# First blocks of a fused Mamba-2 scan and ELU layer: exponents from three bf16 parts, a shorter first load, a later state

## The chip, the cores and the metric

The kernel runs on one core of a Trainium2 chip. A core has TensorE (matrix products, "PE" in the profile, its weight loads "PEld"), VectorE ("DVE"), ScalarE ("ACT"), GpSimd ("POOL"), and SyncE ("SP"), which here issues nearly all DMA transfers. The metric is the device time of one execution in microseconds (us), median of three. The profile describes one execution and has its own clock: its span runs from the first to the last instruction.

## The reference

First a state-space scan over 4 batches, 8 heads and 768 tokens, with head dimension 32 and state dimension 16, in chunks of 32 tokens; then a two-layer network with ELU over the 3072 tokens (256 to 2048 to 256).

```python
log_a = np.log(np.clip(a, 1e-06, 1.0))
for c in range(nc):                                  # chunks of one sequence
    cum = np.cumsum(la, axis=-1)
    L = np.exp(cum[..., :, None] - cum[..., None, :]) * causal
    M = np.einsum('bhin,bhjn->bhij', Cc, Bc) * L
    y_intra = np.einsum('bhij,bhjd->bhid', M, xc)
    y_inter = np.einsum('bhin,bhnd->bhid', Cc, state) * np.exp(cum)[..., None]
    y[:, :, sl] = y_intra + y_inter
    decay_from_j = np.exp(cum[..., -1:] - cum)
    state = np.exp(np.sum(la, -1))[..., None, None] * state + sum_j(Bc * xc * decay_from_j)
h = x @ w_in                                         # x is y, heads side by side
g = np.where(h > 0.0, h, np.exp(np.minimum(h, 0.0)) - 1.0)
out = g @ w_out
```

The result does not depend on the chunk length. The weights come as 64-bit floats and are made 32-bit on the chip.

## The kernel before: the parts concerned

The kernel uses chunks of 64 tokens (`Q`) and blocks of 256 tokens of one batch, so there are 12 blocks. Index `u` is a half block of 128 tokens, `v` a chunk in it, `q` a pair of heads. All instructions stand in the order in which the program writes them; each engine takes its own in that order.

The logarithm of a, its running sum within chunks (`F[:, 0]`), the exp of that (`F[:, 1]`), and the decay to the end of a chunk (`E`) are made once for all blocks, on 96 rows (the last 32 of 128 repeat the first):

```python
la = const.tile([P, 2, P], F32, name="la")
for k, g in enumerate((0, 1, 2, 0)):
    (nc.scalar if k % 2 else nc.sync).dma_start(out=la[BH * k:BH * (k + 1)], in_=...)   # cut
...
nc.vector.tensor_scalar(out=la, in0=la, scalar1=1e-6, scalar2=1.0, op0=ALU.max, op1=ALU.min)
nc.scalar.activation(la, la, ACT.Ln)
nc.vector.tensor_tensor_scan(out=F[:, 0]..., data0=keep..., data1=la..., ...)           # cut
nc.scalar.activation(F[:, 1], F[:, 0], ACT.Exp)
nc.vector.tensor_tensor(out=E..., in0=F_uv[:, :, Q - 1:Q].to_broadcast(...), in1=F_uv, op=ALU.subtract)
nc.scalar.activation(E, E, ACT.Exp)
```

The exponents of L for blocks 0 and 1 are made on TensorE, in a PSUM bank for each half of the heads, from a mask (`first_low`), plus the running sum along one axis (`first_cum`), minus it along the other (`first_minus`), in 32-bit products of 32 rows; `first_decay` takes their exp. Later blocks get L through a copy in DRAM (`write_flat`, `spread_cum`) and 16 small exps (`decay`).

```python
def first_cum(*which):
    for k in range(4):
        for n, hh, r in which:
            row, rows = 32 * r + rows_of(n).start % 32 + 4 * hh + k, slice(32 * r, 32 * r + 32)
            for v in range(2):
                nc.tensor.matmul(out=st[n]["x", hh][Q * v:Q * v + Q, k],
                    lhsT=ident[rows, row:row + 1].to_broadcast([32, Q]),
                    rhs=F[rows, 0, :, Q * v:Q * v + Q], ...)

def first_minus(*which):
    for u in range(2):
        for n, hh, r in which:
            ...
            nc.tensor.matmul(out=st[n]["x", hh][:, :, u], lhsT=F[rows, 0, u],
                rhs=minus[rows, r0:r0 + 4].unsqueeze(2).to_broadcast([32, 4, Q]), ...)
```

The other steps of a block: `turned(E, "eb", ...)` turns E so that tokens are rows; `scaled` multiplies B by it on GpSimd (`sc`); `turn` turns B and C on TensorE (`bt`, `ctm`); `first_exp` spreads `F[:, 1]` (`ec`), which `turn_exp` multiplies into C (`cts`); `sums` makes the chunks' additions to the state, `states` the states (`S_new` on VectorE, masked `Sx` on GpSimd); `scores` makes C times B in four banks; `weigh(n, q)` multiplies a bank by L (`M`, VectorE); `across` and `inside` make y in four banks, and end with ScalarE's copies to `yT`.

```python
def weigh(n, q):
    M = att.tile([P, 2, 2, Q], F32, tag="M", name="M", bufs=8)
    nc.vector.tensor_tensor(out=M, in0=s["g"][q], in1=s["L"][:, 2 * q:2 * q + 2]..., op=ALU.mult)
```

The network: `l1(n, i)` makes two of 16 column blocks of the hidden layer, `elu()` its ELU (two ScalarE passes over `e`, one VectorE operation that writes `g` and is the last reader of the PSUM bank), `l2(n, j)` the second layer.

```python
def l1(n, i):
    ps = psum([P, 2, BLK], "ps_h")
    for j in range(2):
        m = 2 * i + j
        for k in range(KC):
            nc.tensor.matmul(out=ps[:, j], lhsT=w_in[:, k, m * P:(m + 1) * P], rhs=yT[n // 2]..., ...)

def elu():
    n, i, ps = lag.pop(0)
    nc.scalar.activation(e, ps, ACT.Relu, scale=-1.0)
    nc.scalar.activation(e, e, ACT.Exp, scale=-1.0)
    nc.vector.scalar_tensor_tensor(out=g_of[n][:, 2 * i:2 * i + 2], in0=e, scalar=1.0, in1=ps,
                                   op0=ALU.subtract, op1=ALU.max)
```

A weight piece is one load of 512 KB (`w_load`), an Abs and a low part on ScalarE (`w_abs`, `w_low`), a sign, a clamp and a shift on VectorE (`w_sign`, `w_high_a`, `w_high_b`), and a sum on GpSimd (`w_sum`). From piece 4 the low part is VectorE's. `l1(n, i)` needs piece i.

[...] Seven form a ring of buffers (tag "a"), taken in turn; one is kept apart for `l2`, the idle products and some sums. The order of the first blocks:

```python
first = (0, 0, 0), (0, 1, 3)
first_low(0, 0); first_low(0, 1); idle_products(3)
first_cum(*first)
eb = turned(E, "eb", 1.0, nc.scalar)
turn(0); first_exp(0); scaled(0, nc.gpsimd); turn_exp(0)
sums(0, pool=p_o, tag="o")
first_minus(*first)
w_abs(0); first_decay(0, 0); w_low(0, nc.scalar); first_decay(0, 1)
states(0)
for _ in range(2):
    psum([P, 4, P], "ps_none")
scores(0)
w_sign(0); w_high(0); w_sum(0)
for q in range(4):
    weigh(0, q)
second = (1, 0, 0), (1, 1, 3)
first_low(1, 0); first_low(1, 1, p_o)
w_abs(1); w_low(1, nc.scalar)
inside(across(0), 0)
w_sign(1); w_high_a(1); w_sign(2); w_high_b(1); w_sum(1)
l1(0, 0)
w_abs(2); w_low(2, nc.scalar); w_give(2)
first_cum(*second); first_minus(*second)
l1(0, 1); elu()
w_abs(3); w_sign(3); w_low(3, nc.scalar)
first_decay(1, 0); first_decay(1, 1)
turn(1); first_exp(1); scaled(1, nc.gpsimd); w_give(3); turn_exp(1)
l1(0, 2); elu()
scores(1)
sums(1, pool=p_o, tag="o")
weigh(1, 0); weigh(1, 1)
elu()
states(1)
weigh(1, 2); weigh(1, 3)
l1(0, 3)
w_take(4, nc.vector)
inside(across(1), 1)
ncum = turned(F[0:ROWS, 0], "ncum", -1.0, nc.vector)
w_give(4); elu()
...                     # loads cut; then l1 of (1, 0), (1, 1), (0, 4), (1, 2), (0, 5), (1, 3), (0, 6),
                        # (1, 4), (0, 7), (1, 5), (1, 6), (1, 7), with block 2 and pieces 5 to 9 between
ends = {(3, 14): 4, (5, 10): 6, (7, 13): 8, (9, 9): 10}   # (block, step) after which y of two blocks is made
```

After that, `l2(n - 2, i)` and `l1(n, i)` alternate for n from 2 to 11, with the scan of the later blocks between.

## Time and profile before

| | us |
|---|---|
| time, median of 3 runs | 387.92 |
| time, lowest and highest | 387.64, 389.07 |
| span of the profiled execution | 385.5 |
| w_in piece 0: issued, landed | 4.7, 9.6 |
| L of block 0: the two exps end | 10.78, 11.91 |
| last products (second half of the second layer, block 11) start | 368.5 |

In a line of the timeline the columns are the start, the time to the end of the group, the engine, the source line, the operation, output and inputs, the count, and, in brackets, how long the engine had been idle and what ended that. A line of groups with a count is a run of equal instructions. A 32-bit matrix product is two records of the trace; a bf16 product is one. The page names `l1` as L538, `l2` as L569, `first_cum` as L368, `first_minus` as L379, `scores` as L417, the yT copies as L521, `weigh` as L426 and the VectorE part of `elu` as L552.

The weights and the scan's inputs are loaded by long runs of small transfers, most of them in the first 60 us:

```profile
w<-in_moe_w_in_dram SPq DMA_DIRECT2D x8, 512.0 KB, 5.2
xr<-in_x_dram SPq DMA_DIRECT2D x24, 128.0 KB, 3.2
bc<-in_B_dram SPq DMA_DIRECT2D x24, 64.0 KB, 3.7
```

The columns are the transfer, the issuing queue, the number of transfers, the size of one, and the median time from issue to landing.

### The profile page before, as it was taken

How to read it: one execution, taken by the hardware profiler on the slowest of the kernel's cores; microseconds unless marked ns; L12 is line 12 of the kernel's file. 1: busy time of each engine (PE TensorE's matmuls, PEld its weight loads, DVE VectorE, ACT ScalarE, POOL GpSimd, SP SyncE). 2: the span in 40 equal slices, each digit the busy share in tenths (PEclk: the TensorE clock that was granted, in tenths of full speed). 3: DMA queues.
4: the chain of work that ended last, by engine and by line, in shares of the span. 5: the costliest groups of instructions: out<-in, count | busy, mean ns of one | idle time of the engine just before them, and what ended most of it. 6: DMA issues, size and time to landing. Idle time of an engine off the chain costs nothing.

```text
span 385.5 us, 8666 instructions
## 1 busy us (share of the span) xinstructions
PE 378.7 (98%) x3544; PEld 324.1 (84%) x3544; DVE 136.9 (36%) x280; ACT 196.7 (51%) x455; POOL 72.1 (19%) x131
## 2 busy tenths in 40 slices
PE   8899999999999999999999999999999999999996
PEld 4678788888888888888888888888888888888885
DVE  4877878932521232611132431123161212221000
ACT  3969969675334576344467335367534333334000
POOL 5525426623200112400022220011310000000000
PEclk9999999999999999999999999999999999999999
DMA  8979956543004505003524002540000000000000
GB/s 173 226 155 263 296 88 148 96 105 94 3 28 57 84 0 138 3 3 61 64 40 136 3 2 41 60 67 29 0 4 2 27 2 23 4 2 28 0 29 27
DMA packets 87176, 25.15 MB, mean 65 GB/s; under 512 B 77312, under 2 KB 81760, under 8 KB 87136
## 3 DMA queue, kind: packets, MB, share of 16 engines
q1 hardware_dynamic: 84960, 24.39, 29.6%
q8 instruction: 28, 0.46, 0.5%
q10 hardware_dynamic: 2176, 0.20, 0.4%
q14 instruction: 12, 0.10, 0.1%
HBM read 21.23 MB, written 3.34 MB: 64 GB/s over the span
## 4 chain that ended last, share of the span: by engine, by line
PE 88%; ACT 4%; DMA 3%; SPq 3%; issue 1%; DVE 0%; ACTq 0%
PE ps_o L569 40%; PE ps_h L538 38%; PE ps_o L585 4%; PE ps_y L508 2%; SPq L111 2%; PE ps_g L417 1%; DMA w<-in_moe_w_in_dram 1%; PE ps_y L490 1%; ACT L L397 1%; DMA xr<-in_x_dram 1%; PE ps_st L445 1%; DMA flat<-F 1%; ACT e L550 1%; SPq L119 1%; ACT mag L156 1%
## 5 line engine op out<-in xcount | busy, mean ns | idle before, releaser
L538 PE MATMUL ps_h<-yT,w_in 128*128 128x256 f32 x768 | 181.4, 380 | 1.4 <-DVE g L552 0.9
L569 PE MATMUL ps_o<-w_out,g 128*128 128x256 f32 x704 | 166.1, 380 | 0.0
L538 PEld LDWEIGHTS ps_h<-yT,w_in 128*128 128x128 f32 x768 | 145.1, 190 | 22.6 <-ACT yT L521 0.9
L569 PEld LDWEIGHTS ps_o<-w_out,g 128*128 128x128 f32 x704 | 132.3, 190 | 18.2 <-POOL L L402 0.2
L552 DVE SCALAR_TENSOR_TENSOR g<-e,ps_h 128x512 f32<-128x512 f32 x96 | 65.9, 686 | 208.3 <-ACT e L551 208.3
L550 ACT ACTIVATE e<-ps_h 128x512 f32<-128x512 f32 x96 | 57.1, 595 | 138.2 <-PE ps_h L538 138.1
L551 ACT ACTIVATE e<-e 128x512 f32<-128x512 f32 x96 | 60.5, 631 | 3.0
L402 POOL TENSOR_SCALAR_AFFINE_SELECT L<-L 64x512 f32<-64x512 f32 x40 | 27.0, 675 | 157.0 <-ACT L L397 155.6
L397 ACT ACTIVATE L<-L,ncum 128x64 f32<-128x64 f32 x160 | 41.8, 333 | 0.0
L521 ACT COPY yT<-ps_y 64x256 f32<-64x256 f32 (+3 forms) x46 | 14.3, 318 | 9.8 <-PE ps_y L508 9.3
L467 POOL TENSOR_TENSOR Sx<-S_new,hmask 128x64 f32<-128x64 f32 x44 | 13.0, 304 | 20.3 <-DVE S_new L462 12.7
L426 DVE TENSOR_TENSOR M<-ps_g,L 128x256 f32<-128x256 f32 x48 | 16.8, 415 | 0.1
L575 ACT COPY ob<-ps_o 128x512 f32<-128x512 f32 x11 | 6.3, 577 | 15.3 <-PE ps_o L569 15.3
L585 PE MATMUL ps_o<-w_out,g 128*128 128x256 f32 x64 | 14.0, 379 | 0.0
L585 PEld LDWEIGHTS ps_o<-w_out,g 128*128 128x128 f32 x64 | 12.2, 190 | 1.7
L198 POOL TENSOR_TENSOR w_in<-mag,w_in 128x512 uint32<-128x512 uint32 x8 | 10.3, 1294 | 15.8 <-DVE mag L188 15.8
L198 POOL TENSOR_TENSOR w_out<-mag,w_out 128x512 uint32<-128x512 uint32 x8 | 10.2, 1275 | 15.4 <-DVE mag L188 15.4
L188 DVE SCALAR_TENSOR_TENSOR mag<-mag,sgn 128x512 uint32<-128x512 uint32 x16 | 12.6, 790 | 0.5
L462 DVE SCALAR_TENSOR_TENSOR S_new<-S_new,ec,ps_st 128x64 f32<-128x64 f32 x40 | 10.9, 279 | 2.1
L156 ACT ACTIVATE mag<-w 128x512 f32<-128x512 f32 x16 | 10.8, 672 | 1.4 <-DMA w<-in_moe_w_in_dram 1.4
L508 PE MATMUL ps_y<-M,xr 64*32 64x64 f32 x768 | 9.6, 225 | 0.0
L342 DVE TENSOR_TENSOR ctm<-ps_tc,hmask 128x512 f32<-128x512 f32 x12 | 8.2, 684 | 3.8 <-PE ps_tc L335 3.8
(66 smaller groups left out, 132.8 us busy)
## 6 DMA issues: line engine op xcount, KB each, us to landing
L<-flat SPq DMA_DIRECT2D x20, 256.0 KB, 4.7
w<-in_moe_w_in_dram SPq DMA_DIRECT2D x8, 512.0 KB, 5.2
w<-in_moe_w_out_dram SPq DMA_DIRECT2D x8, 512.0 KB, 6.0
xr<-in_x_dram SPq DMA_DIRECT2D x24, 128.0 KB, 3.2
out_dram<-ob SPq DMA_DIRECT2D x11, 256.0 KB, 2.2
bc<-in_B_dram SPq DMA_DIRECT2D x24, 64.0 KB, 3.7
bc<-in_C_dram SPq DMA_DIRECT2D x22, 64.0 KB, 3.0
ec<-flat_exp SPq DMA_DIRECT2D x72, 16.0 KB, 1.7
```

What stands on the lines that cost most here:

```text
L156: nc.scalar.activation(w_mag[i].bitcast(F32), w_words(i)[1].bitcast(F32), ACT.Abs)
L198: nc.gpsimd.tensor_tensor(out=w, in0=w_mag[i][:, :, cols], in1=w, op=ALU.add)
L397: nc.scalar.activation(L[:, h, u], L[:, h, u], ACT.Exp, bias=ncum[:, u, row:row + 1])
L402: nc.gpsimd.affine_select(out=part, in_=part, pattern=[[0, 4], [0, 2], [1, Q]], compare_op=ALU.is_ge, fill=0.0, base=0, channel_multiplier=-1)
L426: nc.vector.tensor_tensor(out=M, in0=s["g"][q], in1=s["L"][:, 2 * q:2 * q + 2].rearrange("p k u i -> p u k i"), op=ALU.mult)
L508: nc.tensor.matmul(out=y[t][v][col:col + D, at, u], lhsT=s["x"][toks, u, D * h:D * (h + 1)], rhs=s["M"][h // 2][toks, u, h % 2], start=Fal ...
L538: nc.tensor.matmul(out=ps[:, j], lhsT=w_in[:, k, m * P:(m + 1) * P], rhs=yT[n // 2][:, k, n % 2].rearrange("p u i -> p (u i)"), start=(k = ...
L550: nc.scalar.activation(e, ps, ACT.Relu, scale=-1.0)
L551: nc.scalar.activation(e, e, ACT.Exp, scale=-1.0)
L552: nc.vector.scalar_tensor_tensor(out=g_of[n][:, 2 * i:2 * i + 2], in0=e, scalar=1.0, in1=ps, op0=ALU.subtract, op1=ALU.max)
L569: nc.tensor.matmul(out=o_of[n][:, ts], lhsT=g_of[n][:, m, ts * P:(ts + 1) * P], rhs=w_out[:, m], start=(m == 0 and ts == 0), stop=(m == MC ...
L585: nc.tensor.matmul(out=ps, lhsT=g_of[n][:, m, ts * P:(ts + 1) * P], rhs=w_out[:, m], start=(m == 0), stop=(m == MC - 1))
```

## The change

The change has five parts. It is meant to let the first y come sooner, and to take work of blocks 0 and 1 out of TensorE's way.

1. The first log a to arrive (`la0`) is that of the first 256 tokens of all rows, loaded four times into the four quarters of the partitions. The full log a follows as one load, and its logarithm, scan, exp and E come later, in the middle of the first blocks.
2. The exponents of blocks 0 and 1 come from `cum16`: bf16(cum) on two quarters of the rows, and the two remainders, each rounded to bf16, on the others. One product over 128 rows adds them up, so `first_cum` and `first_minus` are bf16 products. Those of block 1 move ahead of `across(0)`.
3. The first weight piece is loaded and converted in two halves of 128 columns.
4. The last state of block 0 (chunk `u = v = 1`) is made after block 1's states, ahead of `l1(0, 3)`.
5. PSUM is eight named banks with one buffer each. The first block's tiles name their banks; later ones follow a ring of seven. The steps at which scores, y and some decays of blocks 4 to 11 are made are changed.

```diff
+    banks = ctx.enter_context(tc.tile_pool(name="banks", bufs=1, space=PSUM))
+    ring = [0]
+    def psum(shape, name, bank=None):
+        if bank is None:
+            bank = ring[0]
+            ring[0] = (bank + 1) % 7
+        return banks.tile(shape, F32, tag=f"bank{bank}", name=name)
...
-    nc.vector.tensor_scalar(out=la, in0=la, scalar1=1e-6, scalar2=1.0, op0=ALU.max, op1=ALU.min)
-    nc.scalar.activation(la, la, ACT.Ln)
...
+    clip(la0)
+    nc.scalar.activation(la0, la0, ACT.Ln)
+    sums_of(F0, la0)
+    nc.scalar.copy(out=cum16, in_=F0[:, 0])
+    from_last(E0, F0[:, 0], nc.vector)
+    nc.scalar.activation(E0, E0, ACT.Exp)
+    low2, low3 = slice(2 * BH, P), slice(3 * BH, P)
+    nc.vector.tensor_tensor(out=left[low2], in0=F0[low2, 0], in1=cum16[low2], op=ALU.subtract)
+    nc.vector.tensor_copy(cum16[low2], left[low2])
+    nc.vector.tensor_tensor(out=cum16[low3], in0=left[low3], in1=cum16[low3], op=ALU.subtract)
+    nc.scalar.activation(F0[:, 1], F0[:, 0], ACT.Exp)
...
+    def first_cum(n, hh):
+        for k in range(4):
+            for v in range(2):
+                nc.tensor.matmul(
+                    out=ps[Q * v:Q * v + Q, k],
+                    lhsT=sel[:, row + k:row + k + 1].to_broadcast([P, Q]),
+                    rhs=cum16[:, :, Q * v:Q * v + Q], ...)
+        for u in range(2):
+            nc.tensor.matmul(
+                out=ps[:, :, u], lhsT=cum16[:, u],
+                rhs=minus[:, row:row + 4].unsqueeze(2).to_broadcast([P, 4, Q]), ...)
...                                        # the new order of the first blocks
+    first_low(0, 0, 0)
+    first_low(0, 1, 1)
+    idle_products(3)
+    eb0 = turned(E0, "eb0", 1.0, nc.scalar, BH, 4)
+    turn(0, (5, 6))
+    first_exp(0, 7)
+    scaled(0, nc.gpsimd)
+    turn_exp(0)
+    sums(0, bank=(4, 5), part=most)
+    for hh in range(2):
+        first_cum(0, hh)
+        first_decay(0, hh)
+    states(0, most)
+    scores(0, bank=(6, 7, 0, 1))
+    w_abs(0, half[0])
+    w_low(0, nc.scalar, half[0])
+    weigh(0, 0)
+    weigh(0, 1)
+    w_sign(0, half[0])
+    w_high(0, half[0])
+    w_sum(0, half[0])
+    weigh(0, 2)
+    weigh(0, 3)
+    clip(la)
+    for hh in range(2):
+        first_low(1, hh, 2 + hh)
+        first_cum(1, hh)
+    w_abs(0, half[1])
+    w_low(0, nc.scalar, half[1])
+    nc.scalar.activation(la, la, ACT.Ln)
+    first_decay(1, 0)
+    inside(across(0, bank=(4, 5, 6, 7)), 0)
+    w_sign(0, half[1])
+    w_high(0, half[1])
+    w_sum(0, half[1])
+    w_abs(1)
+    w_sign(1)
+    w_high_a(1)
+    w_low(1, nc.scalar)
+    w_sign(2)
+    w_high_b(1)
+    w_sum(1)
+    sums_of(F, la)
+    nc.scalar.activation(F[:, 1], F[:, 0], ACT.Exp)
     l1(0, 0)
+    first_decay(1, 1)
     w_abs(2)
     w_low(2, nc.scalar)
     w_give(2)
-    first_cum(*second)
-    first_minus(*second)
     l1(0, 1)
     elu()
...                                        # block 1 as before, up to:
     weigh(1, 2)
     weigh(1, 3)
+    st[0] = kept
+    sums(0, bank=(None, 7), part=last)
+    states(0, last)
     l1(0, 3)
     w_take(4, nc.vector)
     inside(across(1), 1)
-    ncum = turned(F[0:ROWS, 0], "ncum", -1.0, nc.vector)
+    from_last(E, F[:, 0], nc.gpsimd)
+    ncum = turned(F[:, 0], "ncum", -1.0, nc.vector, ROWS)
+    nc.scalar.activation(E, E, ACT.Exp)
+    eb = turned(E, "eb", 1.0, nc.scalar, ROWS)
     w_give(4)
     elu()
...
-    ends = {(3, 14): 4, (5, 10): 6, (7, 13): 8, (9, 9): 10}
+    ends = {(3, 8): 4, (5, 10): 6, (7, 6): 8, (9, 10): 10}
+    scores_at = {4: 1, 6: 2, 8: 0, 10: 2}
```

## The prediction

> **What bounds the kernel now.** I read the granted clock first (1.000 on the one core, so nothing is throttled), then the page's first part, then a table of busy time by stage, then the timeline of the first 54 us.
>
> ```profile
> PE 378.7 (98%) x3544; PEld 324.1 (84%) x3544; DVE 136.9 (36%) x280; ACT 196.7 (51%) x455; POOL 72.1 (19%) x131
> ```
>
> 98% says little by itself, because matmul ends are modelled. The chain of waits has 1.73 us for each group of 8 records of the two large layers. There are 12 x 8 groups of each layer, so 192 x 1.73 = 332 us of the 385.5 us is work that nothing here changes. The stage table shows where the rest lies (columns: stretch, length, busy time and count of PE, PEld, DVE, ACT, POOL, clock, DMA share, GB/s):
>
> ```profile
> 0.00:13.65 13.65, 11.11 (x214) 6.30 (x215) 7.95 (x23) 7.55 (x17) 7.25 (x25) 1.00 0.86 179
> 13.65:27.43 13.78, 13.54 (x232) 10.48 (x232) 10.66 (x23) 9.48 (x21) 5.90 (x8) 1.00 0.87 205
> 27.43:53.40 25.97, 24.96 (x262) 20.60 (x263) 19.79 (x43) 21.89 (x54) 12.06 (x15) 1.00 0.93 238
> 53.40:368.50 315.10, 315.10 (x2773) 274.74 (x2772) 98.47 (x193) 156.41 (x364) 46.90 (x83) 1.00 0.22 42
> ```
>
> From 53.4 us on TensorE never idles, so the retimed scores and ends of the later blocks can gain nothing there; they can only cost. Everything is decided by when TensorE reaches the first l2, at 53.42 us. Before that, ScalarE is busy 21.89 of 25.97 us and DVE 19.79: those queues, not TensorE alone, set the pace. The timeline's landmarks (start, duration, engine, line, operation):
>
> ```profile
> 11.40 1.41 DVE L426 TENSOR_TENSOR M<-ps_g,L 128x256 f32<-128x256 f32 x4
> ...
> 13.68 1.97 PE L538 MATMUL ps_h<-yT,w_in 128*128 128x256 f32 x8 [0.21 <-ACT yT L521]
> ...
> 15.57 1.10 PE L368 MATMUL ps_x<-F,ident 32*64 32x128 f32 x32
> ...
> 16.61 1.14 PE L379 MATMUL ps_x<-minus,F 32*128 32x256 f32 x8
> ...
> 17.67 1.99 PE L538 MATMUL ps_h<-yT,w_in 128*128 128x256 f32 x8
> ...
> 22.20 0.69 PE L417 MATMUL ps_g<-ctm,bt 32*64 32x128 f32 x32
> ...
> 23.36 1.99 PE L538 MATMUL ps_h<-yT,w_in 128*128 128x256 f32 x8
> ...
> 26.57 1.64 ACT L521 COPY yT<-ps_y 128x128 f32<-128x128 f32 x6 [2.43 <-PE ps_y L508]
> ```
>
> These are the path to the fourth l1 and beyond: between 13.68 and 23.36 us TensorE does three l1 groups, the exponents of block 1 and its scores, with hardly a gap. From the chain of waits, in the third stage:
>
> ```profile
> 43.03 0.70 DVE g L552
> 43.73 0.14 issue
> 43.87 1.97 PE ps_h L538 x8
> ```
>
> Here TensorE stood still until a g had been read out of PSUM.
>
> [...] So I go through the changed queues by hand, in order, with the durations of this trace. The trace agrees: the g of l1(1,3) ends at 43.73 us and the l1 that needs its PSUM bank starts at 43.87. [...]
>
> **The change, part by part.**
>
> *Removed:* the exponents of block 1 (first_cum and first_minus, 15.57 to 17.67 us, 2.10 us) no longer stand between l1(0,0) and l1(0,1). In bf16 they are 16 + 4 records instead of 32 + 8 per block[...]. They move into the wait for M of block 0. Gain: 2.1 us.
>
> *Start of block 0.* E0 is turned first: its exp ended at 5.99 before, and 32 exponent records stood ahead of the turn (6.52). So sc comes 0.4 us sooner. Both exps of L run before the weight piece and end near 9.9 us, not 11.91. But the third and fourth bank of the scores are now the banks that these exps read, so the scores end near 10.6 us and M starts at 10.7 (before 11.40). DVE then does two M (0.70), the three operations on half a piece (0.9), two M (0.70) and the clip of the full log a (0.32): 13.3 us. ScalarE has the log of it in front of the yT copies: log 0.42, an exp of L 0.57, two copies 0.39, 0.15 to TensorE: l1(0,0) at 14.8 us, against 13.68: +1.1. Halving the load brings nothing: the built program's first Abs waits for both halves.
>
> *Weights 1 and 2.* Abs of piece 1 now stands behind the yT copies (done 15.0): Abs 0.58, clamp, sign of piece 2 and shift 1.46, sum on POOL 1.28: l1(0,1) at 18.4 (17.67 before). The scan (0.69) is behind it on DVE, ScalarE waits for it at 17.75, then exp of F and of L, Abs: 19.25; DVE 1.1; POOL 1.28: l1(0,2) at 21.7, against 20.2. The 2.1 us gain is gone: +1.5.
>
> *Block 1's scores.* ScalarE goes on: low part 0.70, elu(0,0) 1.25, piece 3 1.25, two copies 0.70, elu(0,1) 1.25, to 24.4; g 0.69: 25.1. By the built program's waits, the third score bank is the bank of l1(0,1), free only with that g. Scores end at 25.7 (22.8 before).
>
> *The last state of block 0.* Its four products stand ahead of l1(0,3) in TensorE's queue and wait for the fourth state of block 1, because they take its bank (7). DVE comes there after two M (0.70), g(0,2) (0.69), one copy and three states (1.1): 28.3. So l1(0,3) starts at 28.4 instead of 23.36: +5.0.
>
> *The full E.* l1(0,3) 1.73, the across products 0.4: the inside products start near 30.6 (26.05 before). Then, in a row: 0.5 to the first yT copy, six copies 1.64, exp of E 0.42, turn on TensorE 0.55, copy of eb 0.32, elu(0,3) 1.25, g 0.69, 0.1: 36.1 us. l1(1,0) waits for all of it, since the ring gives it the bank of l1(0,3). Before, it started at 27.43 with a second stop to 28.26, in effect 27.8. So +8.3.
>
> *One bank further.* From l1(1,0) to the first l2 took 25.6 us before (27.8 to 53.42). The ring now stands one place further, so the scores of block 2 wait for g(1,3), which takes 15.9 us as before, and l1(1,5) waits for g(1,4). On DVE g(1,3) to g(1,4) took 43.73 to 49.20, 5.5 us, with a weight piece, four M and four states between. So l1(1,5) at 21.5 us after l1(1,0), then two groups 3.45, y 1.25, one group 1.73: 27.9 us. That is +2.3. Sum: 8.3 + 2.3 = +10.6 us, or 398.5. I take half a microsecond off for waits that overlap: **398.0 us**.
>
> **Rivals.** (1) The change does what it is meant to do: the 2.1 us of exponents fall away and the head is no later, near 386 us. For it: TensorE idles in the head (11.11 busy of 13.65). Against: the weight pieces behind it need ScalarE, DVE and POOL in that order. (2) The losses overlap, and only the wait on bank 7 and the full E remain, 2.0 + 3.8 us, less the 2.1: near 392. For it: ScalarE idles 4.1 of the 26 us to 53.4. Against: that idle time lies near 48 to 51 us, after the pace is set. (3) The later blocks stall too, as their scores now come 2.5 l2 and l1 pairs (8.6 us) before the ends that need them, against 7.4 us of M, states and g on DVE: up to 2 us more, 400. Before, block 6 had the same distance at no cost, so I give it little.
>
> **Range and chances.** Each link of this working is good to a tenth or two, some forty of them: about 1.5 us, and more on the low side, where an unexpected overlap would fall. Range 393.5 to 400.5. The 2% line is 395.7; I give 0.78 that it is passed, 0.21 that the time is within 2%, 0.01 for faster.
>
> **What would show it.** Right: no exponents of block 1 after l1(0,0); l1(0,0) near 14.8; TensorE idle of about 2 us ahead of the last four state products, near 26 to 28; about 4 us idle ahead of l1(1,0), near 32 to 36, ended by a g; l1(1,5) waiting for a g; the first l2 near 64; full from there on. Wrong: if l1(0,3) starts before 25 us, the bank 7 wait is misread; if l1(1,0) starts within 2.5 us of the inside products, the chain through E is; if the span between the first l2 and the end is over 333 us, the later blocks stall.

## The result, and the profile after

The changed kernel took 404.0 us (median; 403.59 to 404.21), the kernel before 387.99 us beside it: the ratio is 1.0407, with a 95% interval of 1.0384 to 1.0429. The change makes the kernel 4% slower. The prediction had the direction and most of the path right, but 404.0 us lies outside its range of 393.5 to 400.5.

The page after, first the busy time of the engines, then the granted TensorE clock in forty slices of the span (9 is 90% or more), then a line of the queues (packets, MB, share of the DMA engines), to which I come back:

```profile
PE 384.6 (96%) x3506; PEld 327.0 (81%) x3506; DVE 138.4 (34%) x288; ACT 198.3 (49%) x462; POOL 73.4 (18%) x135
...
PEclk9986799999999999999999999999999999999999
...
q8 instruction: 27, 0.44, 0.5%
```

TensorE has 38 records fewer than before (3506 against 3544) and is still 5.9 us longer busy. That suggests that some of its products ran slower, and the second line says where: the clock was not full in slices 3 to 5, which are 20 to 50 us. In the profiled execution of the kernel before, it was 1.000 throughout.

The timeline of TensorE after, up to the first l2 (start, time to the end of the group, engine, line, operation, count, and in brackets the idle time and what ended it; L586 is `l1`, L617 `l2`, L463 `scores`, L492 `sums`, L556 `inside`, L332 `turned`):

```profile
15.26 1.97 PE L586 MATMUL ps_h<-yT,w_in 128*128 128x256 f32 x8 [0.93 <-ACT yT L569]
19.12 1.99 PE L586 MATMUL ps_h<-yT,w_in 128*128 128x256 f32 x8 [1.89 <-POOL w_in L213]
...
22.16 1.99 PE L586 MATMUL ps_h<-yT,w_in 128*128 128x256 f32 x8 [0.18 <-POOL w_in L213]
...
25.12 0.68 PE L463 MATMUL ps_g<-ctm,bt 32*64 32x128 f32 x28 [0.60 <-DVE g L600]
...
28.49 0.44 PE L492 MATMUL ps_st<-xr,sc 64*32 64x64 f32 x8 [2.28 <-DVE S_new L509]
28.86 3.78 PE L586 MATMUL ps_h<-yT,w_in 128*128 128x256 f32 x8
...
33.23 1.21 PE L556 MATMUL ps_y<-M,xr 64*32 64x64 f32 x64
...
36.07 0.39 PE L332 MATMUL ps_eb<-ident,E 96*128 96x96 f32 x2 [1.31 <-ACT E L751]
38.84 13.43 PE L586 MATMUL ps_h<-yT,w_in 128*128 128x256 f32 x48 [2.38 <-DVE g L600]
...
63.18 3.69 PE L586 MATMUL ps_h<-yT,w_in 128*128 128x256 f32 x16 [2.10 <-DVE g L600]
...
69.87 1.89 PE L617 MATMUL ps_o<-w_out,g 128*128 128x256 f32 x8
```

Two things are to be read here. The waits are the predicted ones: pieces of w_in ahead of l1(0,1) and l1(0,2), the last state's products 2.28 us behind a state (`S_new`), l1(1,0) 2.38 us behind a g. But two groups are too long. One l1 takes 1.97 to 1.99 us to its modelled end; the one at 28.86, which is l1(0,3), takes 3.78. And six of them in a row should take 5 x 1.73 + 1.97 = 10.6 us; those at 38.84 take 13.43. Nothing in a bracket explains that, since a slow instruction is not a wait. The windows of TensorE alone show it (stretch, length, busy time and count of PE, granted clock, DMA share, GB/s):

```profile
26.00:28.00 2.00, 0.21 (x28) 0.87 1.04 301
28.00:30.00 2.00, 1.51 (x11) 0.50 0.99 99
...
32.00:34.00 2.00, 2.00 (x81) 0.50 1.05 287
34.00:36.00 2.00, 0.76 (x32) 0.92 1.02 237
36.00:38.00 2.00, 0.39 (x2) 0.93 0.97 307
38.00:40.00 2.00, 1.16 (x3) 0.50 1.01 326
...
44.00:46.00 2.00, 2.00 (x9) 0.86 1.03 333
```

The clock is exactly one half in two stretches. If a window of 2 us has a mean of 0.87, 0.13 x 2 / 0.5 = 0.52 us of it was at half clock; so the first fall is at 27.5 us and the rise at 34.3, the second at 37.7 and 44.6. Each lasts about 6.8 us. Each begins some 1.3 us after TensorE fell idle, in the two longest gaps of this part: the wait ahead of the last state's products, and the wait ahead of l1(1,0). The work done at half clock is l1(0,3) (3.78 for 1.99), the across and inside products (0.66 for 0.42 in the kernels that were at full clock here, and 1.21 for 0.88) and the first two l1 behind the second gap, in the 5.7 us from 38.84 to 44.6 (13.43 for 10.63): about 1.8 + 0.2 + 0.3 + 2.8 = 5.1 us.

The chain of waits after (start, duration, engine and line) shows what the second gap ends with: the turned E is copied, and only then come the ELU of l1(0,3) and the g that frees the bank.

```profile
36.49 0.32 ACT eb L335
36.81 0.51 ACT e L598
37.34 0.64 ACT e L599
38.01 0.70 DVE g L600
```

The kernel before, at the same two places:

```profile
27.43 11.03 PE L538 MATMUL ps_h<-yT,w_in 128*128 128x256 f32 x48 [0.18 <-ACT yT L521]
...
53.42 1.89 PE L569 MATMUL ps_o<-w_out,g 128*128 128x256 f32 x8
```

The first l2 starts at 69.87 us (53.42 before), and from there to the end of the span it is 332.2 us (332.1 before). So all 16.45 us are lost ahead of the first l2, and the retimed scores and ends of the later blocks cost nothing here.

### The profile page after: what moved, and what is told of

Read it like the earlier page. It is cut to its first block, busy times and chain, and to the rows that moved or that the text cites. A ratio compares the mean times of both kernels' runs of the same rounds, so it can differ in the third digit from the quotient of the medians.

```text
span 402.1 us, 8603 instructions
## 1 busy us (share of the span) xinstructions
PE 384.6 (96%) x3506; PEld 327.0 (81%) x3506; DVE 138.4 (34%) x288; ACT 198.3 (49%) x462; POOL 73.4 (18%) x135
## 4 chain that ended last, share of the span: by engine, by line
PE 90%; DVE 4%; SPq 2%; ACT 2%; issue 1%; POOL 1%; DMA 0%; ACTq 0%; DVEq 0%; POOLq 0%
PE ps_h L586 39%; PE ps_o L617 38%; PE ps_o L633 3%; PE ps_y L556 2%; PE ps_g L463 2%; SPq L359 1%; PE ps_y L538 1%; PE ps_idle L230 1%; PE ps_st L492 1%; DVE g L600 1%; DVE M L472 1%; PE ps_tb L388 1%; SPq L129 0%; DVE S_new L509 0%; PE ps_tc L388 0%
## 5 line engine op out<-in xcount | busy, mean ns | idle before, releaser
L586 PE MATMUL ps_h<-yT,w_in 128*128 128x256 f32 x768 | 186.1, 388 | 7.5 <-DVE g L600 4.5
L586 PEld LDWEIGHTS ps_h<-yT,w_in 128*128 128x128 f32 x768 | 148.0, 194 | 30.0 <-issue 6.0
L617 PE MATMUL ps_o<-w_out,g 128*128 128x256 f32 x704 | 165.9, 380 | 0.0
L617 PEld LDWEIGHTS ps_o<-w_out,g 128*128 128x128 f32 x704 | 132.5, 190 | 18.1 <-POOL L L448 0.2
L514 POOL TENSOR_TENSOR Sx<-S_new,hmask 128x64 f32<-128x64 f32 x44 | 12.9, 304 | 36.5 <-DVE S_new L509 20.2
L213 POOL TENSOR_TENSOR w_in<-mag,w_in 128x512 uint32<-128x512 uint32 (+1 forms) x9 | 10.6, 1182 | 27.1 <-DVE mag L203 25.9
L203 DVE SCALAR_TENSOR_TENSOR mag<-mag,sgn 128x512 uint32<-128x512 uint32 (+1 forms) x17 | 11.9, 698 | 0.6
L170 ACT ACTIVATE mag<-w 128x512 f32<-128x512 f32 (+1 forms) x17 | 10.9, 640 | 0.0
L463 PE MATMUL ps_g<-ctm,bt 32*64 32x128 f32 x384 | 8.9, 279 | 1.6 <-DVE g L600 1.3
L463 PEld LDWEIGHTS ps_g<-ctm,bt 32*64 32x64 f32 x384 | 6.3, 130 | 4.8 <-issue 4.0
```

Of the source, the lines that this page charges most:

```text
L213: nc.gpsimd.tensor_tensor(out=w, in0=w_mag[i][:, :, cols], in1=w, op=ALU.add)
L463: nc.tensor.matmul(out=gs[q][toks, at, u], lhsT=s["bt"][rows, u, toks], rhs=s["ctm"][rows, u, :, toks], start=True, stop=True, tile_positi ...
L617: nc.tensor.matmul(out=o_of[n][:, ts], lhsT=g_of[n][:, m, ts * P:(ts + 1) * P], rhs=w_out[:, m], start=(m == 0 and ts == 0), stop=(m == MC ...
```

## The experiments

Four groups: what the waits cost, what the clock costs, whether the later blocks' schedule costs anything, and whether the new parts can be arranged so that they do not cost. My theory after the result: the three waits of the prediction (bank 7 behind a state, E and its turn ahead of the ELU, the order of banks) hold, and half clock behind the gaps is what I left out. The rivals: the clock is only a symptom and the waits alone were mis-sized; or the time lies in the later blocks.

### The waits one by one

**The last state made early, as before.** All four states in the head; an unused tile keeps the ring's place, so that no bank changes.

```diff
-    sums(0, bank=(4, 5), part=most)
+    sums(0, bank=(4, 5))
-    states(0, most)
+    states(0)
...
-    st[0] = kept
-    sums(0, bank=(None, 7), part=last)
-    states(0, last)
+    psum([P, 4, P], "ps_none")
```

> Block 0's fourth state goes back to the head with the other three; the place in the ring of PSUM banks that its late products took stays taken, so the banks of all later tiles are the changed kernel's. Theory (waits in the queues, and the clock falling to half after a gap): the 2.28 us idle ahead of those products is gone, l1(0,3) starts near 26.4 us (28.86) at full clock, the inside products of block 1 wait for its last M instead, near 29.2 us (33.23), and everything behind is 4 us sooner: 400.0 us; the second gap, ahead of l1(1,0), stays with its slow records. Rival 1 (waits alone, the long records are not a matter of the gap): l1(0,3) still takes 3.8 us and 2.3 us are gained at most: 401.7. Rival 2 (another wait takes its place, the g or the M of block 1): within 1 us of 404.0.

401.84 us, ratio 1.0352 (1.0329 to 1.0374). The time alone would fit rival 1 (401.7); the trace does not. TensorE's timeline in this run:

```profile
27.07 1.97 PE L586 MATMUL ps_h<-yT,w_in 128*128 128x256 f32 x8 [1.09 <-DVE S_new L507]
...
30.82 0.85 PE L556 MATMUL ps_y<-M,xr 64*32 64x64 f32 x61 [1.14 <-issue]
...
36.40 11.98 PE L586 MATMUL ps_h<-yT,w_in 128*128 128x256 f32 x48 [2.38 <-DVE g L600]
```

l1(0,3) starts 1.8 us sooner and, with a gap of only 1.09 us ahead of it, at full clock: 1.97 instead of 3.78. That makes 3.6 us by 29 us. Of these, 2.4 are left at l1(1,0): a stop of 1.14 us within the inside products, which nothing in the trace releases ("issue"), takes the rest. The gap ahead of l1(1,0) is 2.38 us as in the changed kernel, for its cause (E) is untouched, and the clock falls there too (11.98 for 10.63). It falls once more behind a wait of 2.10 us ahead of l1(1,5), which left it up in the changed kernel: two groups take 5.38 us there instead of 3.69. That takes 1.7 us back. The same happens in six of the runs below (the turn early, both, the head's order, the 24 large fillers and the two runs with small ones); beside the changed kernel, their gains look about 1.7 us too small.

**E turned early.** The exp of E and its turn move ahead of the last state; the last state stays late.

```diff
+    from_last(E, F[:, 0], nc.gpsimd)
+    nc.scalar.activation(E, E, ACT.Exp)
+    eb = turned(E, "eb", 1.0, nc.scalar, ROWS)
     st[0] = kept
...
     ncum = turned(F[:, 0], "ncum", -1.0, nc.vector, ROWS)
-    nc.scalar.activation(E, E, ACT.Exp)
-    eb = turned(E, "eb", 1.0, nc.scalar, ROWS)
```

> The exp of the full E and its turn go ahead of block 0's last state, where ScalarE stood idle from 26.0 us on; nothing else. l1(1,0) then takes the turn's PSUM bank, free long before, and waits only for the yT copies. Theory: l1(1,0) near 35.7 us instead of 38.84, and with the gap ahead of it only about 1 us, no second fall of the clock: the six groups of l1 take 10.4 us instead of 13.4, so 404.0 - 3.1 - 2.7 = 398.2 us. Rival 1 (waits alone): 404.0 - 3.1 = 400.9. Rival 2 (g(0,3), which l1(1,1) now needs, or weight piece 4 takes the wait over): over 402.5.

401.62 us, 1.034 (1.0325 to 1.0355): 3.4 us slower than expected. The subtraction that makes E is on GpSimd, and in its queue it stood behind the masked states of block 1 (in the changed kernel four of these run from 27.40 to 28.72 us, the fifth from 29.35, and E starts at 29.72). So the turn waited 3.58 us for E on TensorE, ahead of the last state's products and of l1(0,3), which starts at 30.45 and runs at half clock (3.78). I had moved one wait to another place. l1(1,0) still starts 2.4 us sooner (36.40), and at full clock, so the turn of block 2 comes 4.1 us sooner; 1.7 of these are lost at l1(1,5), as above.

**Both**, without the unused tile, so that the banks of later tiles differ by one place.

> Both at once, without the extra place in the ring: fourth state in the head, exp and turn of the full E ahead of l1(0,3). Theory: l1(0,3) waits only for g(0,2), near 27.2 us, inside products near 29.5, l1(1,0) near 32.0 (28.3 in the kernel before, 38.84 in the changed one), the clock stays at 1.00 throughout, and the scores of block 2 and l1(1,5) keep their waits for a g: first l2 between 58 and 60, so 392 to 394.5 us. Rival (losses overlap with something that neither touches, the weights of pieces 1 to 4 or block 1's scores): over 396.

400.86 us, 1.0318 (1.029 to 1.0347), where I had expected 392 to 394.5. The same wait, now with nothing behind it to hide it:

```profile
29.53 0.58 PE L332 MATMUL ps_eb<-ident,E 96*128 96x96 f32 x2 [3.56 <-ACT E L742]
```

l1(0,3) starts at 29.90, later than in the changed kernel, and takes 3.67 us. l1(1,0) still starts 3.1 us sooner (35.75). Moving the turn alone does not take the two waits away: in these runs E itself comes too late for it.

**Only the banks.** Nothing moves; the turned E goes to the bank kept apart, so that l1(1,0) needs no bank of l1(0,3), and most of the third stage's tiles get the banks that the pool gave them before.

```diff
-    eb = turned(E, "eb", 1.0, nc.scalar, ROWS)
+    eb = turned(E, "eb", 1.0, nc.scalar, ROWS, 7)
+    r = [(ring[0] + k) % 7 for k in range(7)]
-        l1(n, i)
+        l1(n, i, {8: r[5], 9: r[1], 10: r[2], 11: r[3]}.get(s))
-            scores(2)
+            scores(2, bank=(r[6], r[1], r[0], r[4]))
...                                  # sums(2) and across(2) get named banks too, then ring[0] = r[1]
```

> The changed kernel with other PSUM banks and the same order of work: the turn of the full E goes to bank 7, outside the ring, so l1(1,0) finds a free bank; and the tiles between l1(1,0) and the first l2 take the banks that they had in the kernel before (the first three score banks of block 2 those of the turn and of exp(cum), l1(1,5) a score bank). Theory (two of the four lost waits are only the rotation of banks): l1(1,0) directly behind the turn, near 36.5 us (38.84), and from there to the first l2 25.6 us, plus 2.7 if the clock still falls in the first gap, so first l2 near 64.8 and 399 us; 396 if it does not fall. Rival 1 (l1(1,0) is held by the work ahead of it on ScalarE, not by its bank): 38.8 as before and under 1 us gained there. Rival 2 (block 2's stretch is paced by ScalarE and DVE, so free banks bring nothing): 28 us or more from l1(1,0) to the first l2.

398.17 us, 1.0248 (1.0224 to 1.0271), near the 399 expected: 5.8 us of the 16 come back.

```profile
35.91 0.39 PE L332 MATMUL ps_eb<-ident,E 96*128 96x96 f32 x2 [1.44 <-ACT E L751]
36.14 1.92 PE L586 MATMUL ps_h<-yT,w_in 128*128 128x256 f32 x8
38.68 8.87 PE L586 MATMUL ps_h<-yT,w_in 128*128 128x256 f32 x40 [0.63 <-DVE g L600]
...
55.91 0.46 PE L492 MATMUL ps_st<-xr,sc 64*32 64x64 f32 x32 [0.99 <-PE ps_h L586]
...
63.73 1.89 PE L617 MATMUL ps_o<-w_out,g 128*128 128x256 f32 x8
```

With another bank, l1(1,0) starts right behind the turn of E: the gap of 2.38 us is gone, and with it the fall of the clock (five groups in 8.87 us, full clock). So part of the 5.8 us is half clock avoided. From the turn of block 2 to the first l2 it takes 16.34 us, against 17.77 in the changed kernel and 15.12 before. So these banks are worth 1.4 us at this place, and more by the gap that the changed kernel's opened. They are not all those of the kernel before: the state products of block 2 took the first score bank there, which an M frees, and here that of l1(0,6), so that they start only behind its g, after the 0.99 us of the line above. From l1(1,0) to the first l2 it takes 27.59 us, where I had expected 25.6.

The clock fell in this run as well, earlier, behind the 1.90 us wait ahead of l1(0,1), which left it up in the changed kernel:

```profile
18.78 2.88 PE L586 MATMUL ps_h<-yT,w_in 128*128 128x256 f32 x8 [1.90 <-POOL w_in L213]
```

By the inside products of block 1 (33.20 against 33.23) the two kernels are level again, because l1(0,3) was shorter (3.23 for 3.78).

**The head's order.** Abs and low part of piece 1 move ahead of the copies of y; the clip and the logarithm of the full a, and the exps of L of block 1, move behind the copies and behind piece 2.

```diff
-    clip(la)
...
+    w_abs(1)
+    w_low(1, nc.scalar)                      # ahead of inside(across(0), 0)
...
+    w_sign(2)
+    clip(la)
+    l1(0, 0)
+    w_abs(2)
+    w_low(2, nc.scalar)
+    first_decay(1, 0)
+    nc.scalar.activation(la, la, ACT.Ln)
+    first_decay(1, 1)
+    w_give(2)
     sums_of(F, la)
```

> Only the head's order is changed: clip and log of the full log a, its running sum and the exps of L of block 1 go behind the copies of y and behind weight piece 2; Abs and low part of piece 1 go ahead of the copies, where ScalarE idled 2.0 us. Theory (queue order is what took the bf16 exponents' gain): l1(0,0) near 14.8 us (15.26), l1(0,1) near 17.2 (19.12), l1(0,2) near 19.8 (22.16), and all behind it up to 2.3 us sooner, so 401.7 us; where the clock falls can move this by 2.7 us either way. Rival (the transfers of pieces 1 and 2 or GpSimd's sums pace l1(0,1) and l1(0,2)): under 0.7 us gained at l1(0,2).

404.77 us, 1.0417 (1.0395 to 1.0438): no gain, where I had expected 2.3 us.

```profile
17.69 1.99 PE L586 MATMUL ps_h<-yT,w_in 128*128 128x256 f32 x8 [1.01 <-POOL w_in L213]
...
20.57 1.99 PE L586 MATMUL ps_h<-yT,w_in 128*128 128x256 f32 x8
...
24.83 0.68 PE L463 MATMUL ps_g<-ctm,bt 32*64 32x128 f32 x28 [1.56 <-DVE g L600]
...
62.13 5.38 PE L586 MATMUL ps_h<-yT,w_in 128*128 128x256 f32 x16 [2.10 <-DVE g L600]
```

l1(0,1) and l1(0,2) start 1.4 and 1.6 us sooner, and then the scores wait 1.56 us for a g instead of 0.60, so that they start at 24.83 instead of 25.12. ScalarE's ELU passes and the g behind them set that place, not the products ahead of it. So of 1.6 us only 0.3 get past the bank of l1(0,1). By the turn of block 2 the run is 1.0 us ahead (51.06 against 52.10), and the fall of the clock at l1(1,5), the last line, takes 1.7 us back. That the time is no better is due to both.

### The clock

To hold the clock without moving any wait, I put products into the gaps whose results nobody reads ("fillers"), on banks that are free there: work is added and none is taken away. They stand before the last state, before the turn of E and before l1(1,0).

**24 large bf16 fillers** (128x512):

```diff
+    def warm(count, bank):
+        ps = psum([P, 4, P], "ps_warm", bank)
+        for _ in range(count):
+            nc.tensor.matmul(out=ps, lhsT=ident16,
+                rhs=ident16.unsqueeze(1).to_broadcast([P, 4, P]), start=True, stop=True)
...
+    warm(9, ring[0])                 # ahead of st[0] = kept
+    warm(5, 7)                       # ahead of the exp and turn of E
+    warm(10, 7)                      # behind it
```

> The changed kernel with all its waits, plus 24 products whose result nobody reads, placed in TensorE's three gaps: 9 ahead of block 0's last state products, 5 between the two turns, 10 ahead of l1(1,0). They are 128x512 in bf16, 0.22 us each at full clock, and fill the gaps of 2.28, 1.31 and 2.38 us. Theory (the clock fell because of the gaps): granted clock 1.00 everywhere, l1(0,3) 1.75 us instead of 3.78, six groups of l1 in 10.4 us, l1(1,0) near 36.6, first l2 near 64.6: 399 us. Rival (the long records come from something else, such as the transfers, whose share is 1.0 in the same stretch, or the clock falls whatever TensorE does): no gain, 404 us or up to 1 us more.

404.34 us, 1.0403 (1.0362 to 1.0444): in time a clear miss. In the trace the clock stays at 1.00 until about 58 us, l1(0,3) takes 1.99 us, the six groups 10.63, and the first l2 is at 66.29, 3.6 us sooner. (Then it falls once, and l1(1,5) and l1(1,6) take 5.38 instead of 3.69. Of the four executions of this kernel, one had a granted clock of 1.000 and took 402.26 us; the profiled one had 0.996 and took 404.11.) But the later blocks take 336.1 us instead of 332.2, and there stand two stops like the one of 1.14 us above, in a part where the changed kernel has none. One of them is here, within the inside products of two blocks:

```profile
119.48 0.34 PE L562 MATMUL ps_y<-M,xr 64*32 64x64 f32 x14 [1.46 <-issue]
```

The other is 1.89 us, at 239.6. No semaphore ends them.

**Sixteen 32-bit fillers instead**, if the kind of product mattered:

> As the run with 24 bf16 fillers, but with fewer and longer ones (128x512 in fp32, about 0.43 us each): 5 ahead of block 0's last state products, 3 between the two turns, 5 ahead of l1(1,0), and 1 and 2 around the state products of block 2, where the clock fell a third time in that run. All waits of the changed kernel stay. Theory (the slow records are the clock's, the 3.4 us that the bf16 fillers gave back in two stops without a releaser belong to the length of TensorE's instruction stream): clock 1.00 throughout, l1(1,0) near 36.4 us, first l2 near 64.6 against 69.87, and 332 us from there: 398.7 us. Rival 1 (stops of that kind come wherever the stream is longer): clock 1.00 and first l2 near 64.6, but 336 us from there and 402 in all. Rival 2 (the clock is not the cause): 404 or more.

409.55 us, 1.0535 (1.0508 to 1.0561). I had mis-sized them: a 32-bit product of 128x512 is two records of 0.456 us, twice what I had taken, so the fillers outlast the gaps. In the gaps the clock held (it fell once at 19.0 us, ahead of the first filler, and l1(0,1) took 3.62 us); in the later blocks there are stops of 1.79 and 1.50 us. That the clock can be held is all that this run shows.

**128 small bf16 fillers** (128x96), to move all later instructions by exactly one packet of instructions, for the reason given below under the stops:

> The fillers once more, now 128 small ones (128x96 in bf16, about 0.045 us each): 47 ahead of block 0's last state products, 28 between the two turns, 53 ahead of l1(1,0). Waits and banks are the changed kernel's. 128 because the stops without a releaser in the two runs with fillers fell where a 16 KB packet of instructions ends inside the small products of a block pair; a packet holds some 128 weight loads with their products, so 128 more records put every later boundary where the changed kernel has it. Theory (half clock costs about 5 us, the stops are late instructions): no stop, clock 1.00 up to 57 us, l1(1,0) near 36.4 us, first l2 near 66.3 (64.6 if the clock does not fall ahead of l1(1,5) this time), 332.4 from there: 400.6 or 399 us. Rival 1 (fillers cost what they bring): 404. Rival 2 (the stops have another cause): again some 3 us in stops in the later blocks, 403 or more.

401.62 us, 1.0356 (1.0341 to 1.0371). The later blocks have no stop, as expected, and take 332.2 us again. But now there is one of 2.22 us within the fillers themselves:

```profile
30.04 0.24 PE L231 MATMUL ps_warm<-ident 128*128 128x96 bf16 x2 [2.22 <-issue]
```

and the first l2, 68.03, is 1.7 us later than expected. The clock held up to 59.7 us and fell there, as in the run with large fillers.

**The same small fillers, laid out anew**, some of them ahead of l1(0,1) so that the packet ends elsewhere:

> As the run with 128 small fillers, laid out otherwise: 38 ahead of l1(0,1), 38 ahead of block 0's last state products, 16 between the two turns, 28 ahead of l1(1,0), 8 ahead of l1(1,5). In the run before, 45 of them in one gap used a packet of instructions up in 2.1 us and the next was 2.2 us late; with 38 in the head the boundary lies in slower work. Waits and banks stay the changed kernel's. Theory (about 5 us of the 16 are half clock): no stop, no fall of the clock, l1(1,0) near 36.4 us, first l2 near 64.6, 332.4 from there: 399 us. Rival (the time that fillers give back is not instructions that come late): 401 or more with clock 1.00 and a stop again.

400.83 us, 1.0313 (1.0273 to 1.0352). No stop anywhere, and yet the first l2 is at 67.78. The reason is in the windows of TensorE, the second of which holds the start of l1(1,0) at 36.30:

```profile
34.00:36.00 2.00, 1.19 (x29) 1.00 0.86 250
36.00:38.00 2.00, 1.70 (x4) 0.56 0.94 326
```

The clock is at half again. I had put 28 small fillers ahead of l1(1,0), and they are done in 1.4 us; the 1.10 us after them, and 0.76 us ahead of the turn of E, are idle. At 60.1 us it falls again, and l1(1,5) and l1(1,6) take 5.41 us. Of the four executions, two had a clock of 0.996 and took 400.2 us, and two had 0.991 and took 401.45 and 401.75.

**Large and small fillers mixed**: 17 large ones to fill the gaps, and 111 small ones, so that there are 128 again.

```diff
+    def warm(small, large, bank): ...  # small: 128x96, large: 128x512
+    warm(18, 0, ring[0])             # ahead of l1(0, 0)
+    warm(43, 0, 7)                   # ahead of l1(0, 1)
+    warm(20, 5, ring[0])             # ahead of st[0] = kept
+    warm(10, 3, 7)                   # ahead of the exp of E
+    warm(20, 6, 7)                   # behind its turn
+            warm(0, 1, 7)            # ahead of sums(2)
+            warm(0, 2, 7)            # behind states(2)
```

> The changed kernel with fillers in all gaps, 17 of 128x512 and 111 of 128x96, 128 records in all: small ones ahead of l1(0,0) and l1(0,1); small and large ones ahead of block 0's last state products, between the two turns and ahead of l1(1,0); large ones around the state products of block 2. Waits and banks stay. Theory (half clock costs 5 of the 16 us; TensorE kept busy enough keeps its clock): granted clock 1.00 from the head to the end, no stop, l1(1,0) near 36.5 us, first l2 near 64.8, 332.4 from there: 399 us. Rival (what the clock takes lies elsewhere, so that without any fall the time stays): 401 or more at clock 1.00.

398.47 us (398.46 to 398.67), 1.0246 (1.0221 to 1.0271), as expected. The granted clock is 0.999 over the profiled execution and 1.000 in the other three, the trace has no fall before the last products are done, and no stop. TensorE's timeline (lines are ten further on: L596 is `l1`, L627 `l2`):

```profile
28.71 1.99 PE L596 MATMUL ps_h<-yT,w_in 128*128 128x256 f32 x8
...
36.37 10.63 PE L596 MATMUL ps_h<-yT,w_in 128*128 128x256 f32 x48
...
57.82 3.72 PE L596 MATMUL ps_h<-yT,w_in 128*128 128x256 f32 x16
...
64.53 1.89 PE L627 MATMUL ps_o<-w_out,g 128*128 128x256 f32 x8
```

All waits of the changed kernel are kept, 128 products are added, and it is 5.5 us faster. l1(0,3) starts where it did (28.71 against 28.86) and is 1.8 us shorter; l1(1,0) starts 2.5 us sooner; the first l2 is at 64.53 instead of 69.87. So half clock costs the changed kernel 5.34 us at the first l2, and that is shown, not argued: the waits were not touched. It also answers the first rival: the waits alone, at full clock, lead to 64.53, where the prediction had 64. And the rival named with the large fillers, that dense transfers slow the products, does not hold: from 36 to 40 us the DMA share is 1.11 here, at full clock, and 0.99 in the changed kernel.

### The later blocks

**The kernel before with the new schedule of the later blocks.**

```diff
-    ends = {(3, 14): 4, (5, 10): 6, (7, 13): 8, (9, 9): 10}
+    ends = {(3, 8): 4, (5, 10): 6, (7, 6): 8, (9, 10): 10}
+    scores_at = {4: 1, 6: 2, 8: 0, 10: 2}
...                                  # and the loop that uses them, as in the changed kernel
```

> The kernel before with only the last part of the change: scores, ends, decays and scaled B of blocks 3 to 11 at the changed kernel's places. Theory (TensorE is never idle there): within 0.5 us of the kernel before, 388 us. Rival (scores now come too close ahead of the ends that need them): up to 2 us more.

392.8 us, 1.013 (1.0077 to 1.0182), where I had expected 388. From the first l2 to the end of the span it is 336.3 us instead of 332.1. Three stops without a releaser (1.43, 1.25 and 0.91 us) are 3.6 of these 4.2; the trace has no wait of TensorE for a g there. The first l2 itself comes at 54.72 instead of 53.42, although the two kernels are the same up to it: two profiled executions of one program can differ by that much in the head. One of the stops on TensorE, and then the transfers of the 0.2 us from 105.2 on (packets, MB, share):

```profile
105.04 1.20 PE L508 MATMUL ps_y<-M,xr 64*32 64x64 f32 x97
...
107.67 0.46 PE L508 MATMUL ps_y<-M,xr 64*32 64x64 f32 x31 [1.43 <-issue]
```

```profile
q8 instruction: 1, 0.02, 33.2%
```

In the middle of a stream of small products a packet of instructions is transferred, and TensorE goes on some 2.3 us later. The same holds for all nine stops in the five kernels that have one: each ends 2.3 to 2.8 us after such a packet began (from 28.2 to 30.82 in the run with the last state early, from 117.0 to 119.48 in the one with large fillers). Such a packet is 16.3 KB (in the changed kernel 27 are 0.44 MB), and the trace also gives the number of instructions from one to the next: from 314.83 to 342.53 and on to 370.15 us, where the last packets of the kernel before begin, TensorE has some 128 records of products with as many weight loads each time. Reckoned from there (an estimate): as many small products with their loads take about 1.6 us (97 of them took 1.20 above), less than the 2.3 us from a packet's start to the next product; those of l1 and l2 take 27.6 to 27.7 us. So the packet would be late only in streams of small products or just behind them (the stop of 0.91 us stands within the l1 that follows inside), and whether it falls there depends on how many instructions stand ahead. The fillers fit: 24 of them, and the stops appear; 128, and the later blocks have none. The changed kernel has the same schedule as this run with another number of instructions ahead, and loses nothing in the later blocks. What no run shows is when a packet is asked for; that it is late is inferred from these times.

### Can the parts be arranged without loss?

Three kernels with some of the changed kernel's parts (the short log a, bf16 exponents, named banks, the later blocks' schedule) in another order, and without the other two: the first weight piece whole, all states in the head. Besides, E is made early, exponents of block 1 stand between the l1, and banks are chosen so that no early tile needs a late g. The core of the last of them:

```diff
+    w_load(0)                                # one load, not two
+    sums(0, bank=(4, 5)); states(0)          # all four
+    scores(0, bank=(6, 7, 2, 3))
...
+    clip(la); l1(0, 0, 2)
+    first_low(1, 1, 1); first_cum(1, 1)
+    w_abs(2); w_low(2, nc.scalar)
+    nc.scalar.activation(la, la, ACT.Ln)
+    l1(0, 1, 3); elu()
...
+    from_last(E, F[:, 0], nc.gpsimd)         # behind turn(1)
+    l1(0, 2, 7)
+    scores(1, bank=(4, 6, 2, 5)); sums(1, bank=(0, 1))
...
+    l1(0, 3, 3)
+    nc.scalar.activation(E, E, ACT.Exp)
+    eb = turned(E, "eb", 1.0, nc.scalar, ROWS, 4)
+    inside(across(1, bank=(4, 6, 7, 0)), 1)
```

**First order.**

> The changed kernel's bf16 exponents and short loads kept, its order and banks changed back where the runs so far point: the first weight piece whole, its Abs ahead of the exps of L as in the kernel before, all four states of block 0 in the head, clip and log of the full log a, its running sum and the full E in places where DVE, ScalarE and GpSimd idled in the kernel before, the turn of the full E between l1(0,2) and the scores of block 1, the second half of block 1's exponents behind l1(0,0), and banks chosen so that no tile waits for a g except l1(0,3). Theory (all the lost time is order and banks, and the 2.1 us of exponents are a true gain): l1(0,0) near 14.0 us, l1(0,1) near 16.0, l1(0,2) near 18.5, l1(0,3) near 22.5, l1(1,0) near 27.3, no fall of the clock, first l2 near 53, so 387 to 388 us, at or just under the kernel before. Rival (the weight pieces through ScalarE, DVE and GpSimd pace the first three l1 whatever stands on TensorE): l1(0,2) near 20 us and 389 to 391.

391.3 us, 1.0095 (1.0077 to 1.0114): 3.3 us above the range that I had expected. l1(1,0) starts at 26.86, 0.6 us sooner than in the kernel before. The loss comes after. The running sums that block 2 needs are written out late (at 26.09 us, 16.84 before), behind three weight loads and block 2's B, C and x in SyncE's queue, and ScalarE waits for them to come back:

```profile
35.23 1.06 ACT L443 ACTIVATE L<-L,ncum 128x64 f32<-128x64 f32 x4 [2.38 <-DMA L<-flat]
```

**Second order**: the sums written ahead of the loads, E's subtraction on VectorE.

> As the reordered version, which lost 3.4 us behind the turn of block 2 because its running sums were written out only at 26.1 us, behind four loads in SyncE's queue, so that ScalarE waited 2.4 us for the L that comes back. Here the writing and the reading back stand ahead of these loads; the full E is made on VectorE right behind the running sum and turned ahead of l1(0,2), whose bank is no longer that of block 1's exponents. Theory: turn of block 2 near 37.5 us, first l2 near 52.8 (53.42 in the kernel before), 386.5 to 387.5 us. Rival (the weights' loads, now later, pace l1(1,0) to l1(0,5)): first l2 later than 54 and 388.5 or more.

389.91 us, 1.0025 (1.0007 to 1.0043), 2.4 us above the range. The subtraction of 96x256 took 1.32 us on VectorE, against 0.56 in the kernel before and 0.61 on GpSimd in the first order; l1(0,3) comes at 24.00 (23.36 before), behind a wait of 1.07 us for a g.

**Third order**: it goes back to GpSimd, block 1's exps behind the ELU.

> As the first reordered version, with the running sums written out early, the exps of F and of L behind the elu of l1(0,1) so that l1(0,3) finds its bank sooner, the turn of the full E behind l1(0,3), and the state products of block 2 in a bank that its first M frees, as in the kernel before. Theory (the exponents' 2.1 us of TensorE become a gain once ScalarE's queue follows): l1(0,2) near 18.8 us, l1(0,3) near 22.2, l1(1,0) near 26.2 (27.43 in the kernel before), turn of block 2 near 37.1, first l2 near 52.4 against 53.42: 386.8 us beside a kernel before of 387.9, ratio 0.997. Rival (the weight pieces set the pace of l1(0,1) to l1(0,5) whatever stands on TensorE): first l2 at 53.4 or later and a ratio of 1.000 or more.

387.49 us against 388.56 for the kernel before: 0.9963 (0.9946 to 0.998). The ratio is as expected (0.997), well inside 2%, and it is the only version that beats the kernel before.

```profile
22.35 1.99 PE L586 MATMUL ps_h<-yT,w_in 128*128 128x256 f32 x8
...
27.12 11.03 PE L586 MATMUL ps_h<-yT,w_in 128*128 128x256 f32 x48 [0.18 <-ACT yT L569]
...
53.67 1.89 PE L617 MATMUL ps_o<-w_out,g 128*128 128x256 f32 x8
```

l1(0,3) starts 1.0 us sooner than before, l1(1,0) 0.3 us, and the first l2 (53.67 against 53.42) no sooner at all: there I had expected 52.4, and the rival 53.4 or later. The two profiles are a poor pair, though: the span of 386.0 us is one of the longer of this kernel's fourteen executions (median 385.5), and the 385.5 us of the kernel before is below all nineteen of its spans in the same round (385.9 to 389.7, median 386.6). In the profile of the run with the later blocks' schedule, whose head is the kernel before's, the first l2 came at 54.72. So a gain of about 1 us ahead of the first l2 is possible, and not shown; where the 0.4% comes from I leave open. What the run does show: the parts that it keeps need not cost anything, and they bring next to nothing. That ScalarE's and VectorE's queues and the weight pieces set the pace to the first l2, and not the products of the exponents, is how I read it; no run took those queues away.

## Why the prediction was right, and where it failed

*Shorter exponents.* Right in kind: they are gone from between l1(0,0) and l1(0,1), and fill the wait for M. They take 0.67 us a half block; the eight pairs with 64 weight columns took 0.35 us together, 44 ns each.

*Start of block 0.* l1(0,0) at 15.26, predicted 14.8; M starts at 11.23, predicted 10.7, since the exps of L ended at 10.41 and not at 9.9; sc comes no sooner (7.33 against 7.35 before), predicted 0.4 us. Small, all on the same side. The 0.9 us for the three VectorE operations on half a piece was an estimate; they ran from 11.90 to 12.84 us. (In six later runs with the same head, l1(0,0) starts between 14.87 and 15.26.)

*Weights 1 and 2.* 19.12 and 22.16, predicted 18.4 and 21.7: the order ScalarE, VectorE, GpSimd was read correctly and its sums were 0.5 to 0.7 us short. (The 20.2 given for l1(0,2) before is 20.38 in the trace.)

*Block 1's scores.* They end at about 25.8 (25.7): the wait for g(0,1) is there, 0.60 us.

*The last state.* Its products start at 28.49 (28.3), l1(0,3) at 28.86 (28.4), behind a state: right.

*The full E.* The chain from the yT copies through the exp, the turn, the ELU and g is there, link by link. l1(1,0) starts at 38.84, predicted 36.1. This is where the prediction left the path, and not by a link: the inside products start at 33.23, predicted 30.6, since l1(0,3) and the across products ran at half clock.

*One bank further.* Waits and size are right: 27.9 us predicted from l1(1,0) to the first l2; at full clock it took 64.53 - 36.37 = 28.2 us, with the scores and l1(1,5) behind a g as predicted (l1(1,5) 21.45 us after l1(1,0), predicted 21.5), and 31.03 in the changed kernel. The reason was worded wrongly. It isn't one place of a shift: the kernel before does not take its seven banks in turn, although I had written so. In the built program, l1(1,0) and the next five l1 have banks 5, 2, 4, 1, 6 and 0, and the scores of block 2 have 3, 2, 5 and 6; the changed kernel goes strictly round. With most of the kernel before's banks given by name, the last part of that stretch shrinks from 17.77 to 16.34 us.

*The step that failed* is the first sentence: I "read the granted clock first (1.000 on the one core, so nothing is throttled)", and then took durations at full clock for groups that stand behind the idle times of 2 and 4 us that I was predicting myself. The clock belongs to the kernel before, which has no such gaps. In place of 1.73 us a group, l1(0,3) and the first two groups behind the second gap took about twice that; it comes to 5.34 us at the first l2 (64.53 with the clock held, 69.87 without), and 5.5 us of time. With the clock held, 398.47 us stands against 398.0 predicted. That this is so close is partly luck: by the two profiles the first l2 comes 11.1 us later than before, where 10.1 were predicted, since the head's links were short and the overlap taken off did not come.

*The rivals.* None is what happened. The first (near 386) needed an order that does not hold up ScalarE's queue; the third order above has it, and came out at 387.49. The second (losses overlap, 392) is refuted by the first l2 with the clock held: the losses added up. The third (later blocks stall) is refuted for this kernel, 332.2 us; that the same schedule on the kernel before lost 4.2 us there is mostly due to stops that move with the number of instructions (3.6 us), and the trace has none of the waits that the rival meant.

What stays open: where the third order's 0.4% lies; and the bf16 exponents and the halved first piece were tried only together with other parts, not alone on the kernel before.

## What to carry to other kernels

When a change opens idle time on TensorE, reckon with half clock behind it: in the eighteen falls here it lasted 3.4 us eleven times and 6.8 us seven times. Two waits of 2.3 and 2.4 us cost 2.3 and 2.8 us more, and the granted clock of the kernel before (1.000) says nothing about that. It is a risk and not a rule: waits of 1.9 and 2.1 us cost nothing more in the changed kernel, and 0.9 and 1.7 us in other runs. Products that nobody reads give that back (5.5 us here), if they fill the gaps. When a tile's bank is chosen by a fixed order, ask for each early tile which late reader frees its bank, and whose queue that reader stands in; a change of banks alone brought 5.8 us, part of it half clock avoided, so it does not add to the 5.5. And work moved out of TensorE's way is worth little while ScalarE's queue sets when the next bank comes free (0.3 us of 1.6 in the run with the head's order).
